# Mixer kernel on one core: the first channel product in half-height tiles, in one section a chunk

## The chip, the cores and the metric

The kernel runs on one core of one Trainium2 chip. The metric is the device time of one execution in microseconds (us). Before the change it is 2170.19 us, the median of three runs (2169.47 to 2170.86).

## The reference, cut to what matters

All tensors are given in float64. x is 8 x 4096 x 192, weight_gen 8 x 4096 x 8 x 7, and the result has the shape of x.

```python
w = softmax(weight_gen)                                  # over the 7 taps
out = sum over k of w[..., k] * x[:, s - 6 + k, group]   # 8 groups of 24 channels
# then, with x = out:
xt = x.transpose(0, 2, 1)
h = np.maximum(xt @ w_tok1, 0.0) @ w_tok2                # 4096 -> 256 -> 4096
u = x + h.transpose(0, 2, 1)
h2 = np.maximum(u @ w_ch1, 0.0) @ w_ch2                  # 192 -> 1536 -> 192
return (u + h2).astype(np.float32)
```

## The kernel before, in words

The tokens of each of the 8 batches are cut into 8 chunks of 512, so there are 64 chunks (g). For each chunk the kernel runs: the attention (a sum of seven weighted, shifted copies of x, on VectorE, called DVE, with DMAs that add into `xa`); `token1`, this chunk's part of the first token product, summed over the batch in `h1s`; once a batch's eight parts are there, `make_h1`; `token2`, the second token product for one chunk, which gives u; `channel1`, the first channel product; and `channel2`, the second, which sums into `acc`. `store` turns the sum and writes it out. Attention and token1 run about a batch ahead of the rest.

To keep float32 precision with fp32r matmuls, an operand is held as a high part and the low rest, and a product is three matmuls: high by high, low by high, high by low. `u_parts` makes these parts of u: a high part by ScalarE (ACT), a low part by DVE.

The 192 channels of u are the rows that a first-product matmul sums over. 128 of them (`a_hi`, `a_lo`) go through full-height matmuls (L578); the other 64 (`c_hi`, `c_lo`, held twice, in rows 0 to 63 and 64 to 127) through half-height ones (L583), of which two, for two different feature blocks, run in the two halves of the array at the same time. The 12 feature blocks of 128 are six pairs; a pair fills one PSUM tile `ph` (two banks). `channel1(g, q)` computes three pairs, q = 0 or 1: 18 full-height matmuls, then 9 pairs of half-height ones. ACT then takes max(ph, 0) into h (L586) and DVE the low rest (L587). Between the two sections of a chunk stands the second product of the section before, 30 full-height matmuls (L599), and a token2 or token1.

PSUM has eight banks: two for `acc`, and three working tiles of two banks (`ps_w`), shared in turn by `ph`, token2's `up` and token1's `th`. ACT copies x into `up` (L527) and u into `acc` (L607) first, so the matmuls add to them.

The order of the work is written out by the program when it is built: a planner keeps a modelled time per engine (`at`), with fixed costs for each piece, and lets TensorE's sections follow each other; `pump` fills DVE and ACT with items of waiting chains (attention, softmax, weight conversions, `u_parts`, output moves) up to a limit; `picks` says which token product comes next. Each engine then executes its queue in that order. The weights come as float64 and are converted on the chip, w1 and the first pieces of the others in a prologue, the rest in the first chunks.

Of the kernel before, what the change touches and what calls it, by code (L numbers as in the profile page):

```python
# [21 lines left out]
def mixer_kernel(ctx: ExitStack, tc: tile.TileContext, x, wg, wt1, wt2, wc1, wc2, out):  # L22
# [185 lines left out]
    def attention(ms):  # L208
# [29 lines left out]
        for ks in (TAPS if ms[0] >= EARLY * NCH else TAPS0):  # L238
# [209 lines left out]
    def convert_channel(which, n, pool=None):  # L448
# [4 lines left out]
        if which == "w1a":  # L453
            cs = slice(n * HF, (n + 1) * HF)
            yield from split(w1a_hi[:, cs], w1a_lo[:, cs], v)
# [91 lines left out]
    def u_parts(m):  # L547
# [3 lines left out]
        a_hi, a_lo, c_hi, c_lo = (late.tile([P, N], F32R, tag=x, name=x) for x in ("a_hi", "a_lo", "c_hi", "c_lo"))  # L551
        yield "gate", 0, lambda: state["channel1"] >= m * NQ
        yield "w", 0, lambda: free["parts"]
        yield "u", 620, lambda: nc.scalar.copy(a_hi, ua)
        yield "u", 620, lambda: nc.scalar.copy(c_hi[c], uc[c])
        yield "v", 610, lambda: nc.vector.tensor_sub(a_lo, ua, a_hi.bitcast(F32))  # L556
        yield "v", 610, lambda: nc.vector.tensor_sub(c_lo[c], uc[c], c_hi[c].bitcast(F32))
        yield "u", 620, lambda: nc.scalar.copy(c_hi[e], uc[c])
        yield "u", 620, lambda: nc.scalar.copy(c_lo[e], c_lo[c].bitcast(F32))

        def last():
            ut[m] = a_hi, a_lo, c_hi, c_lo
# [6 lines left out]
    def channel1(g, q):  # L569

        a_hi, a_lo, c_hi, c_lo = ut[g]
        pairs = range(PQ * q, PQ * (q + 1))
        ph = {p: ps_w.tile([P, 2, 512], F32, tag="w", name="ph") for p in pairs}
        for p in pairs:
            for j in range(2):
                fs = slice((2 * p + j) * P, (2 * p + j + 1) * P)
                for n, (w, u) in enumerate(((w1a_hi, a_hi), (w1a_lo, a_hi), (w1a_hi, a_lo))):
                    nc.tensor.matmul(ph[p][:, j, :], w[:, fs], u, start=n == 0, stop=False)  # L578
        for p in pairs:
            for n, (w, u) in enumerate(((w1c_hi, c_hi), (w1c_lo, c_hi), (w1c_hi, c_lo))):  # L580
# [9 lines left out]

    def channel2(g, q):
        acc = acc_t[g]
        for p in range(PQ * q, PQ * (q + 1)):
            h = ht.pop((g, p))
            for j in range(2):
                f = 2 * p + j
                for n, steps in ((1, ((C_HL, 0), (C_HL, 1))), (0, ((A_HI, 0), (A_LO, 0), (A_HI, 1)))):
                    for i, (d, l) in enumerate(steps):
                        nc.tensor.matmul(acc[:, n, :], w2s[:, f, d], h[:, j, l, :], start=False,  # L599
                                         stop=f == NF - 1 and i == len(steps) - 1, skip_group_check=True)  # L600
# [155 lines left out]
    def next_lo():
# [303 lines left out]
```

## Time and profile before

| what | value |
|---|---|
| median of three runs | 2170.19 us |
| profiled execution | 2166.28 us |
| its span, first to last instruction | 2164.5 us |
| TensorE busy | 2110.9 us (98%) |
| DVE busy | 1542.7 us (71%) |
| ACT busy | 1274.6 us (59%) |
| mean granted TensorE clock, share of full speed | 0.994 |

PE is TensorE's matmuls and PEld its weight loads, which run beside them. A busy share is a mean over the whole span, and TensorE's records overlap where matmuls are pipelined, so a matmul's pace is read from the starts of successive ones. In the timeline, successive equal instructions are one row with their count; the time of the row is from the first start to the last end.

### The profile page before, as it was taken

The page shows a single profiled execution, that of the slowest core. Times are in us where ns is not written, and L with a number is a line of the kernel's source. Part 1 is how long each engine was busy: PE and PEld are TensorE (multiplying, and loading weights), DVE is VectorE, ACT ScalarE, POOL GpSimd, SP SyncE. Part 2 cuts the span into 40 slices and gives each one's busy share as a digit, 9 for nine tenths or more (in the row PEclk, how much of TensorE's full clock was granted, in tenths as well). Part 3 has the DMA queues.
Part 4 walks back from the last instruction along what each step waited for, and adds up shares of the span by engine and source line. Part 5 has one row for each costly group of instructions (what it writes and reads, how often), then busy time and mean ns, then how long its engine had stood idle before and what let it go on. Part 6 is the DMA issues. An engine that isn't in the chain of part 4 may idle for free.

```text
span 2164.5 us, 27209 instructions
## 1 busy us (share of the span) xinstructions
PE 2110.9 (98%) x10438; PEld 1678.7 (78%) x10438; DVE 1542.7 (71%) x1749; ACT 1274.6 (59%) x1972; POOL 166.5 (8%) x202
## 2 busy tenths in 40 slices
PE   7988999899999999999999999999999999999998
PEld 5766788678778788878887888888788878877776
DVE  8988887788887887777777778777778764343342
ACT  5566664556655655665665566556656655655554
POOL 0001111000100010000100010000000000000000
PEclk9999999999999999999999999999999999999999
DMA  8666768777876677655766676566667553222211
GB/s 277 228 215 199 188 166 235 236 223 197 219 212 182 183 201 194 174 155 171 195 176 185 181 185 154 176 187 184 182 174 199 148 166 107 69 68 69 58 38 22
DMA packets 165826, 366.66 MB, mean 169 GB/s; under 512 B 16456, under 2 KB 104264, under 8 KB 150336
## 3 DMA queue, kind: packets, MB, share of 16 engines
q1 hardware_dynamic: 138304, 285.74, 41.2%
q0 software_dynamic: 26496, 77.61, 18.7%
q8 instruction: 82, 1.34, 0.2%
q10 hardware_dynamic: 896, 1.57, 0.2%
q14 instruction: 48, 0.39, 0.1%
HBM read 225.13 MB, written 70.52 MB: 137 GB/s over the span
## 4 chain that ended last, share of the span: by engine, by line
PE 86%; DVE 6%; DMA 3%; ACT 3%; issue 1%; POOL 0%; SPq 0%; ACTq 0%; DVEq 0%; POOLq 0%
PE acc L599 36%; PE ph L578 21%; PE ph L583 12%; PE up L533 6%; PE tapsum L342 3%; PE th L499 3%; PE th L501 1%; PE th L516 1%; DVE pr L215 1%; DVE h L587 1%; DMA xa<-pr 1%; DMA xs<-t 1%; DMA xt<-in_x_dram 1%; ACT h L586 1%; DVE pr L229 1%
## 5 line engine op out<-in xcount | busy, mean ns | idle before, releaser
L599 PE MATMUL acc<-h,w2s 128*128 128x512 f32 x3840 | 908.5, 393 | 0.0
L599 PEld LDWEIGHTS acc<-h,w2s 128*128 128x128 f32 x3840 | 711.0, 188 | 189.9 <-issue 45.7
L587 DVE SCALAR_TENSOR_TENSOR h<-ph,h 128x1024 fp32r<-128x1024 f32 x384 | 452.9, 1216 | 254.8 <-ACT h L586 252.4
L586 ACT ACTIVATE h<-ph 128x1024 fp32r<-128x1024 f32 x384 | 379.9, 1025 | 389.9 <-PE ph L583 225.4
L578 PE MATMUL ph<-a_hi,w1a_hi 128*128 128x512 f32 x768 | 303.8, 396 | 16.6 <-DVE uf L545 7.7
L215 DVE TENSOR_TENSOR pr<-xt,wn 128x768 f32<-128x768 f32 x336 | 309.2, 947 | 8.5 <-DMA xa<-pr 8.5
L578 PE MATMUL ph<-a_lo,w1a_hi 128*128 128x512 f32 x768 | 300.5, 391 | 1.1 <-DVE a_lo L556 1.1
L578 PE MATMUL ph<-a_hi,w1a_lo 128*128 128x512 f32 x768 | 300.4, 391 | 0.0
L233 POOL DMA_DIRECT2D xa<-pr x176 | 153.0, 870 | 1420.5 <-DVE pr L229 1195.0
L626 ACT COPY out_tile<-oa 32x256 f32<-32x256 f32 x512 | 206.7, 404 | 6.2
L607 ACT COPY acc<-uf 128x1024 f32<-128x1024 f32 x64 | 65.1, 1018 | 246.0 <-DVE oc L617 246.0
L578 PEld LDWEIGHTS ph<-a_hi,w1a_hi 128*128 128x128 f32 x768 | 145.1, 189 | 50.9 <-DVE uf L545 11.7
L578 PEld LDWEIGHTS ph<-a_lo,w1a_hi 128*128 128x128 f32 x768 | 144.7, 188 | 32.8 <-DVE a_lo L556 2.6
L533 PE MATMUL up<-w,h 128*128 128x512 f32 x630 | 157.2, 397 | 10.4 <-ACT up L527 10.4
L578 PEld LDWEIGHTS ph<-a_hi,w1a_lo 128*128 128x128 f32 x768 | 145.2, 189 | 27.9
L583 PE MATMUL ph<-c_hi,w1c_hi 64*128 64x512 f32 x768 | 165.1, 427 | 0.0
L229 DVE TENSOR_TENSOR pr<-pr 128x768 f32<-128x768 f32 x160 | 152.5, 953 | 3.5
L583 PE MATMUL ph<-c_lo,w1c_hi 64*128 64x512 f32 x768 | 151.8, 392 | 0.0
L583 PE MATMUL ph<-c_hi,w1c_lo 64*128 64x512 f32 x768 | 149.9, 387 | 0.0
L533 PEld LDWEIGHTS up<-w,h 128*128 128x128 f32 x630 | 120.3, 192 | 37.1 <-ACT up L527 12.0
L583 PEld LDWEIGHTS ph<-c_hi,w1c_hi 64*128 64x128 f32 x768 | 71.7, 183 | 56.2 <-issue 44.5
L545 DVE TENSOR_TENSOR uf<-up,uf 64x512 f32<-64x512 f32 x63 | 43.0, 683 | 99.0 <-ACT uf L541 99.0
(82 smaller groups left out, 2043.6 us busy)
## 6 DMA issues: line engine op xcount, KB each, us to landing
w<-s SPq DMA_DIRECT2D x96, 1024.0 KB, 5.1
xa<-pr POOLq DMA_DIRECT2D x176, 384.0 KB, 4.9
xt<-in_x_dram SPq DMA_DIRECT2D x56, 960.0 KB, 7.7
out_dram<-out_tile SPq DMA_DIRECT2D x128, 192.0 KB, 2.5
xs<-t SPq DMA_DIRECT2D x58, 384.0 KB, 3.9
xb<-xs SPq DMA_DIRECT2D x348, 64.0 KB, 4.1
raw<-in_moe_w_tok_dram SPq DMA_DIRECT2D x16, 1024.0 KB, 6.0
s<-w POOLq DMA_DIRECT2D x8, 1024.0 KB, 6.3
```

Source lines behind the costliest of these rows:

```text
L215: nc.vector.tensor_mul(t.rearrange("p t (h g) -> p (t h) g", h=H).rearrange("p (o n) g -> p o n g", o=1), x_k, w)
L229: nc.vector.tensor_add(sums[m], sums[m], prt.pop(m))
L233: nc.gpsimd.dma_start(xat[m].rearrange("p t d -> p (t d)"), sums[m].rearrange("p t d -> p (t d)"), accum_op=ALU.add)
L342: nc.tensor.matmul(ps[:, n, 0:half * D], ident, prs[k][:, n * half:(n + 1) * half, :], start=k == 0, stop=k == K - 1)
L533: nc.tensor.matmul(up[:, n, :], h1[:, k, d], w[:, l, k * N:(k + 1) * N], start=k == 0 and j == 0 and not seeded, stop=k == KR - 1 and j == ...
L578: nc.tensor.matmul(ph[p][:, j, :], w[:, fs], u, start=n == 0, stop=False)
L583: nc.tensor.matmul(ph[p][:, j, :], w[rows, p * P:(p + 1) * P], u[rows], start=False, stop=n == 2)
L586: nc.scalar.activation(h[:, :, 0, :], ph[p], AF.Relu)
L587: nc.vector.scalar_tensor_tensor(h[:, :, 1, :], ph[p], 0.0, h[:, :, 0, :].bitcast(F32), op0=ALU.max, op1=ALU.subtract)
L599: nc.tensor.matmul(acc[:, n, :], w2s[:, f, d], h[:, j, l, :], start=False, stop=f == NF - 1 and i == len(steps) - 1, skip_group_check=True)
L607: nc.scalar.copy(acc_t[g], uft.pop(g))
L626: nc.scalar.copy(dst, src[to:to + Q].rearrange("p (n e d) -> p n e d", n=2, d=Q)[:, n])
```

## The change

All 192 channels go through half-height matmuls, as three blocks of 64. `u_parts` puts them into `u_hi` and `u_lo`, three columns of 512 with rows 0 to 63 and 64 to 127 holding the same three blocks, the first two swapped between the halves; w1 is laid out to match. A pair is now 9 x 2 half-height matmuls. All six pairs of a chunk stand in one section. Four h tiles take pairs 0 to 3 at once; pairs 4 and 5 stay in PSUM until the second product has used the first two h tiles (`take_h`). One token product, token2 of the next chunk if it is ready, comes behind the section; then the second product's six pairs, with another token product in their middle. The planner's costs and limits for these pieces are new. The split of taps 5 and 6 for the second batch is gone. Lines of the changed kernel are numbered anew: the first product is L576, the second L594, token2 L527, token1 L493 and L495 (L510 in the first two batches), the seed of up L521, Relu L582 and the low rest L583.

```diff
-    TAPS0 = [(0,), (1, 2), (3, 4), (5,), (6,)]
...
-    w1a_hi = const.tile([P, F], F32R, name="w1a_hi")
-    w1a_lo = const.tile([P, F], F32R, name="w1a_lo")
-    w1c_hi = const.tile([P, F // 2], F32R, name="w1c_hi")
-    w1c_lo = const.tile([P, F // 2], F32R, name="w1c_lo")
+
+
+    w1_hi = const.tile([P, 3, F // 2], F32R, name="w1_hi")
+    w1_lo = const.tile([P, 3, F // 2], F32R, name="w1_lo")
+    TURN = (0, 1, 2), (1, 0, 2)
...
-        for ks in (TAPS if ms[0] >= EARLY * NCH else TAPS0):
+        for ks in TAPS:
...
+        if which == "w1":
+            dst = raw[:, 0:HF, :].rearrange("p (k q n) l -> p k q (n l)", k=3, q=NC1)
+            src = wc1.rearrange("(k c) (q j n) -> k j c q n", k=3, q=NP, j=2)[:, :, :, NC1 * n:NC1 * (n + 1)]
             for j in range(2):
-                nc.sync.dma_start(
-                    raw[j * DC:(j + 1) * DC, 0:HF, :].rearrange("p (q n) l -> p q (n l)", q=NP),
-                    wc1[DA:D].rearrange("c (q j n) -> c q j n", q=NP, j=2)[:, :, j, :])
+                for k in range(3):
+                    nc.sync.dma_start(dst[j * DC:(j + 1) * DC, k], src[TURN[j][k], j])
...
-        yield "u", 620, lambda: nc.scalar.copy(a_hi, ua)
-        yield "u", 620, lambda: nc.scalar.copy(c_hi[c], uc[c])
-        yield "v", 610, lambda: nc.vector.tensor_sub(a_lo, ua, a_hi.bitcast(F32))
-        yield "v", 610, lambda: nc.vector.tensor_sub(c_lo[c], uc[c], c_hi[c].bitcast(F32))
-        yield "u", 620, lambda: nc.scalar.copy(c_hi[e], uc[c])
-        yield "u", 620, lambda: nc.scalar.copy(c_lo[e], c_lo[c].bitcast(F32))
+        yield "u", 620, lambda: act(hi[:, 0], ua)
+        yield "u", 620, lambda: act(hi[c, 2], uc[c])
+        yield "v", 610, lambda: dve(lo[:, 0], ua, hi[:, 0].bitcast(F32))
+        yield "v", 610, lambda: dve(lo[c, 2], uc[c], hi[c, 2].bitcast(F32))
+        yield "u", 620, lambda: act(hi[c, 1], ua[e])
+        yield "u", 620, lambda: act(hi[e, 1], ua[c])
+        yield "u", 620, lambda: act(hi[e, 2], uc[c])
+        yield "u", 620, lambda: act(lo[c, 1], f[e, 0])
+        yield "u", 620, lambda: act(lo[e, 1], f[c, 0])
+        yield "u", 620, lambda: act(lo[e, 2], f[c, 2])
...
-    def channel1(g, q):
-
-        a_hi, a_lo, c_hi, c_lo = ut[g]
-        pairs = range(PQ * q, PQ * (q + 1))
-        ph = {p: ps_w.tile([P, 2, 512], F32, tag="w", name="ph") for p in pairs}
-        for p in pairs:
+    def channel1(g, p):
+
+        u_hi, u_lo = ut[g]
+        ph = ps_w.tile([P, 2, 512], F32, tag="w", name="ph")
+        steps = [(w, u, k) for w, u in ((w1_hi, u_hi), (w1_lo, u_hi), (w1_hi, u_lo)) for k in range(3)]
+        for n, (w, u, k) in enumerate(steps):
             for j in range(2):
-                fs = slice((2 * p + j) * P, (2 * p + j + 1) * P)
-                for n, (w, u) in enumerate(((w1a_hi, a_hi), (w1a_lo, a_hi), (w1a_hi, a_lo))):
-                    nc.tensor.matmul(ph[p][:, j, :], w[:, fs], u, start=n == 0, stop=False)
-        for p in pairs:
-            for n, (w, u) in enumerate(((w1c_hi, c_hi), (w1c_lo, c_hi), (w1c_hi, c_lo))):
-                for j in range(2):
-                    rows = slice(j * DC, (j + 1) * DC)
-                    nc.tensor.matmul(ph[p][:, j, :], w[rows, p * P:(p + 1) * P], u[rows], start=False, stop=n == 2)
-        for p in pairs:
-            h = ht[g, p] = late.tile([P, 2, 2, N], F32R, tag="h", name="h", bufs=5)
-            nc.scalar.activation(h[:, :, 0, :], ph[p], AF.Relu)
-            nc.vector.scalar_tensor_tensor(
-                h[:, :, 1, :], ph[p], 0.0, h[:, :, 0, :].bitcast(F32), op0=ALU.max, op1=ALU.subtract
-            )
-
-    def channel2(g, q):
+                rows = slice(j * DC, (j + 1) * DC)
+                nc.tensor.matmul(ph[:, j, :], w[rows, k, p * P:(p + 1) * P], u[rows, k], start=n == 0,
+                                 stop=n == len(steps) - 1)
...
+    def take_h(g, p, ph):
+        h = ht[g, p] = late.tile([P, 2, 2, N], F32R, tag="h", name="h", bufs=HB)
+        nc.scalar.activation(h[:, :, 0, :], ph, AF.Relu)
+        nc.vector.scalar_tensor_tensor(
+            h[:, :, 1, :], ph, 0.0, h[:, :, 0, :].bitcast(F32), op0=ALU.max, op1=ALU.subtract
+        )
...
-    C1, C2 = 6570, 6820
-    LAST = 690
-    FIRST = 1362
+    PAIR, C2 = 2065, 2272
+    TIGHT4 = 900
+    TIGHT = 1100
...
+    for g in range(NG):
+        phs, kept = {}, {}
+        soon = ((convert_w2, 1),) if g == 0 else ()
+        for p in range(NP):
+            if g == 0 and p == 2 * NC1:
+                need(lambda: ("w1", 2) in done)
+            if p < HB:
+                slack = TIGHT if p < NP // 2 else TIGHT
+                pump(next_lo() + slack, soon, first_h() + slack - TIGHT)
+            phs[p] = channel1(g, p)
+            end = on("pe", PAIR, w_at.popleft(), free["u"] if p == 0 else 0.0)
+            if p < HB:
+                take_h(g, p, phs[p])
+                w_at.append(on("dve", LOW, on("act", TOP, end)))
+                if p == 0:
+                    h_at = w_at[-1]
+            else:
+                kept[p - HB] = end + T2 + (p - HB + 1) * C2 + TOP + LOW
+                w_at.append(kept[p - HB])
+        picked = list(picks(g, 100, 1))
+        state["channel1"] = g + 1
+        state["rest"] = NP * C2
+        free["parts"] = end
+        run_picked(picked)
+        for p in range(NP):
+            if p == NP // 2:
+                if not picked:
+                    if g < NCH - 1 and state["token2"] <= g:
+                        need(lambda: g + 1 in w2t, (convert_w2, g + 1))
+                    picked = list(picks(g, 2000, 2))
+                if not picked:
+                    pump(at["pe"] + SLACK)
+                    picked = list(picks(g, 100, 2))
+                run_picked(picked)
+                if g == 0:
                     need(lambda: ("c2", 2) in done, (convert_channel, "c2", 2))
...
+            channel2(g, p)
+            on("pe", C2, free["acc"] if p == 0 else 0.0, h_at)
+            state["rest"] -= C2
+            if p + HB < NP:
+                pump(at["pe"] + TOP + SLACK, soon, at["pe"])
+                last = p + HB == NP - 1
+                if last:
+                    it = picks(g, (NP // 2 - p - 1) * C2, 2)
+                    picked = list(islice(it, 1))
+                take_h(g, p + HB, phs[p + HB])
+                h_at = on("dve", LOW, on("act", TOP, at["pe"]))
+                if kept[p] in w_at:
+                    w_at[w_at.index(kept[p])] = h_at
+                if last:
+                    picked += list(it)
+                    h_at = 0.0
+        pump(at["pe"] + SLACK_M)
+        need(lambda: state["stored"] >= g - 1, ("o", g - 1))
+        items = store(g)
+        next(items)
+        free["acc"] = on("dve", 1400, at["pe"] + HOP, stored_at.get(g - 1, 0.0))
+        chains.insert(3, Chain(items, 0.0, ("o", g)))
...
```

The first place is TensorE's queue in a chunk of the fourth batch, before: the end of one section's half-height matmuls, the second product, token2 and the start of the next section.

```order
L583 MATMUL ph<-c_hi,w1c_hi 128x512 x2
L583 MATMUL ph<-c_hi,w1c_lo 128x512 x2
L583 MATMUL ph<-c_lo,w1c_hi 128x512 x2
L599 MATMUL acc<-h,w2s 128x512 x30
L533 MATMUL up<-w_7112,h_6987 128x512 x10
L578 MATMUL ph<-a_hi,w1a_hi 128x512
```

The same queue after, in the same batch: the last pair of the section, token2, the second product and token1.

```order
L576 MATMUL ph<-u_hi,w_hi 128x512 x6
L576 MATMUL ph<-u_hi,w_lo 128x512 x6
L576 MATMUL ph<-u_lo,w_hi 128x512 x6
L527 MATMUL up<-w_8132,h_8056 128x512 x10
L594 MATMUL acc<-h,w2s 128x512 x30
L493 MATMUL th<-xh,w_7834 128x384
L495 MATMUL th<-xh,w_7834 128x192
```

Token2 has moved ahead of the second product, and TensorE changes between half and full height twice a chunk instead of four times.

The second place is DVE's queue in a chunk of that batch, before, from the transposes of the store (L616, L617) over token2's last step (L545) and attention steps (L215, L229) to the three low rests of a section.

```order
L616 STREAM_TRANSPOSE oa<-acc 128x512
L617 STREAM_TRANSPOSE oc<-acc 128x512
L619 TENSOR_TENSOR oc<-oc 64x512
L545 TENSOR_TENSOR uf<-up,uf 64x512
L229 TENSOR_TENSOR pr<-pr 128x768
L215 TENSOR_TENSOR pr<-xt,wn 128x768 x2
L229 TENSOR_TENSOR pr<-pr 128x768
L181 TENSOR_REDUCE mx<-wg 128x64
L182 TENSOR_TENSOR wg<-wg,mx 128x448
L587 SCALAR_TENSOR_TENSOR h<-ph,h 128x2x512 x3
```

After, in the fuller of the two kinds of chunk that alternate there (in the other, nothing stands between the first three low rests):

```order
L611 STREAM_TRANSPOSE oa<-acc 128x512
L612 STREAM_TRANSPOSE oc<-acc 128x512
L614 TENSOR_TENSOR oc<-oc 64x512
L214 TENSOR_TENSOR pr<-xt,wn 128x768 x2
L583 SCALAR_TENSOR_TENSOR h<-ph,h 128x2x512
L228 TENSOR_TENSOR pr<-pr 128x768
L583 SCALAR_TENSOR_TENSOR h<-ph,h 128x2x512
L214 TENSOR_TENSOR pr<-xt,wn 128x768
L583 SCALAR_TENSOR_TENSOR h<-ph,h 128x2x512
L214 TENSOR_TENSOR pr<-xt,wn 128x768
L583 SCALAR_TENSOR_TENSOR h<-ph,h 128x2x512
```

Four low rests instead of three stand behind the store, with an attention step between them, and token2's last step (now L539) has moved behind them.

The third place is TensorE's queue at the end of chunk 7, where the second batch's token1 is completed; before and after.

```order
L599 MATMUL acc<-h,w2s 128x512 x30
L516 MATMUL th<-xa,val 128x192 x16
L533 MATMUL up<-w_2379,h_2789 128x512 x10
L578 MATMUL ph<-a_hi,w1a_hi 128x512
L578 MATMUL ph<-a_hi,w1a_lo 128x512
```

```order
L594 MATMUL acc<-h,w2s 128x512 x30
L510 MATMUL th<-xa,val 128x192 x8
L527 MATMUL up<-w_2717,h_3157 128x512 x10
L576 MATMUL ph<-u_hi,w_hi 128x512 x6
L576 MATMUL ph<-u_hi,w_lo 128x512 x6
```

Token2 stands directly ahead of the next first product in both; one token1 instead of two stands ahead of it.

## Rows read from the trace of the kernel before

**Rows 1.** The page: busy shares, chain by line, two groups (busy us, mean ns).

```profile
PE 2110.9 (98%) x10438; PEld 1678.7 (78%) x10438; DVE 1542.7 (71%) x1749; ACT 1274.6 (59%) x1972; POOL 166.5 (8%) x202
...
PE acc L599 36%; PE ph L578 21%; PE ph L583 12%; PE up L533 6%; PE tapsum L342 3%; PE th L499 3%; PE th L501 1%; PE th L516 1%; DVE pr L215 1%; DVE h L587 1%; DMA xa<-pr 1%; DMA xs<-t 1%; DMA xt<-in_x_dram 1%; ACT h L586 1%; DVE pr L229 1%
...
L587 DVE SCALAR_TENSOR_TENSOR h<-ph,h 128x1024 fp32r<-128x1024 f32 x384 | 452.9, 1216 | 254.8 <-ACT h L586 252.4
L586 ACT ACTIVATE h<-ph 128x1024 fp32r<-128x1024 f32 x384 | 379.9, 1025 | 389.9 <-PE ph L583 225.4
```

**Rows 2.** Stretches: us, busy of PE, PEld, DVE, ACT, POOL; granted clock, DMA.

```profile
118.00:426.00 308.00, 283.79 (x1366) 223.09 (x1364) 249.29 (x289) 186.82 (x279) 38.42 (x47) 0.97 0.73 203
426.00:750.00 324.00, 317.66 (x1598) 254.11 (x1596) 264.40 (x310) 195.96 (x306) 32.02 (x37) 1.00 0.73 202
750.00:1750.00 1000.00, 1000.00 (x5039) 805.43 (x5036) 749.59 (x877) 597.54 (x939) 86.44 (x100) 1.00 0.65 180
```

**Rows 3.** TensorE's waits: total us, times, longest us.

```profile
PE up L533 <- ACT up L527: 10.4, 4, 4.5
PE ph L578 <- DVE uf L545: 7.7, 8, 1.7
```

**Rows 4.** TensorE's timeline, steady part: start us, us, instruction.

```profile
1499.83 0.39 PE L578 MATMUL ph<-a_lo,w1a_hi 128*128 128x512 f32 x1
1500.14 0.50 PE L583 MATMUL ph<-c_hi,w1c_hi 64*128 64x512 f32 x2
1500.48 0.40 PE L583 MATMUL ph<-c_hi,w1c_lo 64*128 64x512 f32 x2
1500.71 0.40 PE L583 MATMUL ph<-c_lo,w1c_hi 64*128 64x512 f32 x2
1500.95 0.40 PE L583 MATMUL ph<-c_hi,w1c_hi 64*128 64x512 f32 x2
...
1502.10 0.40 PE L583 MATMUL ph<-c_lo,w1c_hi 64*128 64x512 f32 x2
1502.43 7.10 PE L599 MATMUL acc<-h,w2s 128*128 128x512 f32 x30
1509.37 0.33 PE L499 MATMUL th<-xh,w 128*128 128x384 f32 x1
1509.54 0.25 PE L501 MATMUL th<-xh,w 128*128 128x192 f32 x1
1509.63 0.36 PE L499 MATMUL th<-xh,w 128*128 128x384 f32 x1
...
1511.87 0.40 PE L578 MATMUL ph<-a_hi,w1a_lo 128*128 128x512 f32 x1
...
1515.51 0.39 PE L578 MATMUL ph<-a_lo,w1a_hi 128*128 128x512 f32 x1
```

**Rows 5.** Timeline of DVE and ACT, 600 to 640 us.

```profile
600.76 1.82 DVE L215 TENSOR_TENSOR pr<-xt,wn 128x768 f32<-128x768 f32 x2
...
605.60 1.02 ACT L527 COPY up<-xb 128x1024 f32<-128x1024 f32 x1 [1.73 <-DVE h L587]
...
610.47 0.71 DVE L616 STREAM_TRANSPOSE oa<-acc 128x512 f32<-128x512 f32 x1
...
611.82 0.69 DVE L619 TENSOR_TENSOR oc<-oc 64x512 f32<-64x512 f32 x1
...
624.37 0.62 ACT L554 CAST a_hi<-uf 128x512 fp32r<-128x512 f32 x1
```

**Rows 6.** TensorE's timeline at the end of chunk 7.

```profile
396.41 2.59 PE L533 MATMUL up<-w,h 128*128 128x512 f32 x10 [2.09 <-ACT up L527]
400.97 0.51 PE L578 MATMUL ph<-a_hi,w1a_hi 128*128 128x512 f32 x1 [1.97 <-ACT a_hi L554]
```

**Rows 7.** SP's timeline in the prologue (it issues DMAs).

```profile
19.70 0.69 SPq L433 DMA_DIRECT2D raw<-in_moe_w_ch_dram  x1
29.03 0.33 SPq L370 DMA_DIRECT2D raw<-in_moe_w_tok_dram  x1
```

More of the change, by code (lines that the diff above doesn't have):

```diff
@@ L35, in mixer_kernel @@
     NP = NF // 2
-    PQ = 3
-    NQ = NP // PQ
+    NC1 = NP // 3
+    HB = 4
     KR = R // P
@@ L452, in convert_channel @@
         v, = out
-        if which == "w1a":
-            cs = slice(n * HF, (n + 1) * HF)
-            yield from split(w1a_hi[:, cs], w1a_lo[:, cs], v)
+        if which == "w1":
+            cs = slice(n * NC1 * P, (n + 1) * NC1 * P)
+            yield from split(w1_hi[:, :, cs], w1_lo[:, :, cs], v.rearrange("p (k m) -> p k m", k=3))
         elif which == "c2":
@@ L591, in channel2 @@
-    def channel2(g, q):
-        acc = acc_t[g]
[L593 to L600, printed above, removed]
+    def channel1(g, p):
[3 more added lines that the diff above has]
+        for n, (w, u, k) in enumerate(steps):
+            for j in range(2):
+                rows = slice(j * DC, (j + 1) * DC)
+                nc.tensor.matmul(ph[:, j, :], w[rows, k, p * P:(p + 1) * P], u[rows, k], start=n == 0,
+                                 stop=n == len(steps) - 1)
+        return ph
@@ new lines, in take_h, with channel2 @@
+    def take_h(g, p, ph):
[4 more added lines that the diff above has]
+        )
+    def channel2(g, p):
+        acc = acc_t[g]
+        h = ht.pop((g, p))
+        for j in range(2):
+            f = 2 * p + j
+            for n, steps in ((1, ((C_HL, 0), (C_HL, 1))), (0, ((A_HI, 0), (A_LO, 0), (A_HI, 1)))):
+                for i, (d, l) in enumerate(steps):
+                    nc.tensor.matmul(acc[:, n, :], w2s[:, f, d], h[:, j, l, :], start=False,
+                                     stop=f == NF - 1 and i == len(steps) - 1, skip_group_check=True)
@@ L752, in first_h @@
     def first_h():
-        return max(at["pe"], *(t - i * FIRST for i, t in enumerate(w_at))) + C1 - (PQ - 1) * LAST
+        return max(at["pe"] + state["rest"], w_at[0]) + PAIR
     def next_lo():
@@ L764, in mixer_kernel @@
              "summed": NCH - 1, "turned": FT - 1, "parts": NCH - 1, "kept": FT - 1, "stored": -1, "out": -1,
-             "done": NCH - 1, "w1": NCH, "channel1": 0}
+             "done": NCH - 1, "w1": NCH, "channel1": 0, "rest": 0}
     def raw_free(tag):
@@ L836, in start @@
             return items
-        between = {1: ("w1a", 0), 3: ("w1c", 0), 5: ("c2", 0)}
+        between = {1: ("w1", 0), 3: ("w1", 1), 5: ("c2", 0)}
         w1_v, w1_it = {}, {}
@@ L891, in mixer_kernel @@
         make_h1(0, th[:, :, 0:D])
-        last = start(convert_channel("w1a", 1))
+        last = start(convert_channel("w1", 2))
         soft = softmaxes()
@@ L908, in mixer_kernel @@
         for j in range(2):
-            nc.tensor.matmul(w[:, j, :], w1a_hi[:, 0:P], w1a_hi[:, 0:512], start=True, stop=True)
+            nc.tensor.matmul(w[:, j, :], w1_hi[:, 0, 0:P], w1_hi[:, 0, 0:512], start=True, stop=True)
     run(u_parts(0))
@@ L967, in token2_ready, with picks @@
             and h1_at[m // NCH] <= at["pe"] + soon
-    def picks(g, soon):
+    def picks(g, soon, most):
         two = token2_ready(g + 1, soon)
@@ L973, in picks, with run_picked @@
             yield do_token2, begin_token2(g + 1)
[L974 removed]
+        if two < most and token1_ready(soon) and ready[0][0] <= g + NCH + (2 if not two else BEHIND):
             yield do_token1, begin_token1()
+    def run_picked(picked):
+        for do, it in picked:
+            do(*it)
+        picked.clear()
     seed(0)
[L978 to L1030 removed]
@@ new lines, in mixer_kernel @@
+    for g in range(NG):
[33 more added lines that the diff above has]
+                if g == 0:
+                    need(lambda: ("c2", 2) in done, (convert_channel, "c2", 2))
+            channel2(g, p)
[20 more added lines that the diff above has]
+        chains.insert(3, Chain(items, 0.0, ("o", g)))
+        if g + 1 == NG:
+            break
+        if state["token2"] < g + 1:
+            while (g + 1) // NCH not in h1t:
+                need(token1_ready, ("w1", state["token1"] + 1), ("x", state["token1"] + 1))
+                do_token1(*begin_token1())
+            need(lambda: g + 1 in w2t and g + 1 in xbt, (convert_w2, g + 1))
+            do_token2(*begin_token2(g + 1))
+        need(lambda: g + 1 in ut, ("u", g + 1))
+        seed(g + 1)
+        free["acc"] = on("act", 1050, free["acc"])
```

77 lines of the change are left out of this document (9 added, 68 removed).

## The prediction

> **What bounds the kernel now.** I read the page first. TensorE is busy for 98% of the span, VectorE (DVE) for 71% and ScalarE (ACT) for 59%, and the chain that ended last runs above all through the second channel product (L599, 36%) and the first (L578 and L583, 33%) [rows 1]. Then I read the busy time by stretch, because a mean hides where TensorE waits. From 750 to 1750 us it is busy 1000 us of 1000: there the time is the TensorE instruction stream and nothing else. From 118 us, where the chunks begin, to 426 us it is idle 24.2 us, and from there to 750 us another 6.3 us [rows 2]. In the first of these the granted clock is 0.97 on average: with two levels, 1.2 and 2.4 GHz, that is some 6% of 308 us, about 18 us, at the lower one, which costs about 9 us. The waits say for whom: longest in total for the ACT copy that seeds token2's PSUM tile, and eight times for DVE's last step of u (L545), on which the first channel product waits [rows 3]. So two things can be gained: TensorE's own slots (everywhere), and the waits before 750 us.
>
> **TensorE's slots.** By a slot I mean what streams 512 columns once: one full-height matmul, or two half-height ones that start together (the rows show them as x2). A chunk has 2 x (18 + 9) = 54 slots of the first product before, and 6 x 9 = 54 after: the multiplication is not made cheaper. A full-height slot takes (1515.51 - 1511.87) / 16 = 0.2275 us, a half-height one (1502.10 - 1500.48) / 7 = 0.2314 us [rows 4]. What differs is how often TensorE changes between the two heights. Into half height: 0.31 us from 1499.83 to 1500.14 is 0.083 over a slot, and 0.34 to the next is 0.109 over. Back: 0.33 from 1502.10 to 1502.43 is 0.099 over, and the thirty L599 slots take 6.94 instead of 30 x 0.2275 = 6.825, 0.115 more [rows 4]. A round trip thus costs 0.406 us. Before there are two a chunk, after one, as the order shows: 64 x 0.406 = 26.0 us gone. Against it, 36 full-height slots a chunk become half-height ones: 36 x (0.2314 - 0.2275) x 64 = 9.0 us added. Net gain 17.0 us.
> The half-height pace in a run of 54 slots is not shown; the trace has runs of nine. From below I bound it by the full-height pace, 0.2275 (gain 26.0 + 64 x 18 x 0.0039 = 30.5), from above by the slowest single step, 0.24 between 1500.71 and 1500.95 [rows 4]: then 64 x (36 x 0.0125 + 18 x 0.0086) = 38.7 us are added and the net is a loss of 12.7. I take 0.2314, the mean, since the steps do not grow towards the end of the nine.
>
> **Where the new order could make TensorE wait, in the steady part.** The three working PSUM tiles now hold six pairs in a row: pair 3 needs the tile of pair 0, and token2's seed (ACT, L521 in the new numbering) needs the tile of pair 3. I set t = 0 at the first half-height slot. Pair p is complete at about 0.3 + 2.08 (p + 1), and the product ends at about 12.7. Take the fuller of the two kinds of chunk, the one whose DVE order is shown. DVE starts its transposes at 0.2; the three steps of the store take 2.04 (610.47 to 611.82 + 0.69) and two attention products 1.82 [rows 5], so the first h step starts at 4.1; each takes 1.22 [rows 1], each attention step between them 0.87, as the second of the two in 1.82 does [rows 5]. The h steps end at 5.3, 7.4, 9.5 and 11.5. Tiles are wanted at 6.4, 8.4 and 10.5, so pairs 3 to 5 start on time with about 1 us to spare. The seed takes 1.02 [rows 5] and ends at about 12.65, against 12.7: just in time. ACT has four Relu passes at 1.02 [rows 1] and two seeds of 1.02 there, 6.1 of 12.7 us, and output moves in the rest. I take no wait; its other bound is one more DVE step of 0.95 in each chunk of this kind.
> What the order gains: token2 now comes directly behind the product, before the 13.6 us of the second product, so u's evictions and casts are long done at the next chunk. The eight waits for L545, 7.7 us [rows 3], go. The four casts that are added (0.62 each [rows 5], 64 x 4 x 0.62 = 159 us on ACT, 59% to 66%) lie in that time at no cost. They cost something where token2 still ends its chunk, below.
>
> **The early part, 118 to 750 us.** Here DVE is 81% busy [rows 2] and also converts the weights. Pairing taps 5 and 6 for the second batch too adds eight adds (0.87 each, 7 us of DVE) and takes eight accumulating DMAs away; none of it is on the path, but DVE has less slack. Going through the DVE queue in its new order with the durations above, I find waits for PSUM tiles of 1 to 4 us in chunks 1 to 5, because DVE enters the product late with weight conversions or attention left over; the old places fall away. In chunk 0 the third part of w1 is now wanted for pair 4 instead of the second half, 2 us later. Chunk 7 still ends in the last token1 and token2 directly before the next product: its waits of 2.09 and 1.97 us [rows 6] stay, and as the first pair's nine slots now need all eight casts, 6 x 0.62 = 3.7 us behind the first two against 8 x 0.23 = 1.9 of slots, it loses 1.9 us more, about 2 more for DVE's backlog behind it, and the 1.9 once more in chunk 0. Together I put the idle time of 118 to 426 us at 18 instead of 24.2 us, the loss by the lower clock at 5 instead of 9 (it is 1.00 in the stretches with fewer waits [rows 2]), and 426 to 750 us at 2 instead of 6.3: 14.5 us gained. This is the weak term; its bounds are nothing and all of it, 0 to 39 us.
> The loads of w1: 18 DMAs instead of 4, of 64 partitions each. At 0.69 us of SP for one, each of three places takes some 3.5 us longer; behind the first of them SP idles from 20.4 to 29.0 us until a buffer comes free [rows 7], so it is hidden. If that cover went, a raw tile would come 3.5 us later, and TensorE's chain in the prologue would see at most that.
>
> **Sum.** 17.0 + 14.5 = 31.5 us. The profiled execution took 2166.3 us (span 2164.5 and 1.8 around it), so it would be 2134.8; the median of the runs is 2170.2, 3.9 above the profiled one, and the forecast on that scale is 2138.7 us.
>
> **Rivals.**
> 1. The slots gain and the waits only move: 2170.2 - 17.0 = 2153. For it: DVE's work in the early part is not less, and it was 81% busy there. Against: the waits for L545 have a cause that the new order removes.
> 2. Slower, by token2's seed. The chain fourth pair, Relu, h step, seed has no slack to spare in the fuller chunks. If DVE comes one step of 0.95 later in all of the 52 chunks with attention work, TensorE waits 49 us in front of token2 (L527) and the kernel takes 2138.7 + 49 = 2188. It decides from 31.5 / 52 = 0.6 us per chunk on. Against: every second chunk's queue has no attention step between its h steps, and DVE idles 25% of the steady part [rows 2].
> 3. The half-height pace does not hold over 54 slots, as each has two loads and two matmuls, four instructions in 0.23 us. Break-even lies at 0.2314 + 31.5 / (64 x 54) = 0.2405 us; at the upper bound of 0.24 the time is 2168, no change. Against: in token1 a load and a matmul fit into 0.09 us (1509.54 to 1509.63 [rows 4]), twice as fast as needed; but that is one step in two, not a long run. The Trainium skill, "TensorE: Matmul & The Clock Gate", Part 2, has a rule that speaks against the change: where the sequencer decodes matmuls itself, it spends about 62 ns on each. The two matmuls of a slot would need 124 ns and stay hidden; only if the loads cost as much would a slot take 0.248 us by that figure, and the kernel about 2196, an estimate. The 0.09 us above is against this.
> 4. Nearly all waits go: 17.0 + 35 = 52 us, 2118.
>
> **How the numbers follow.** The forecast has 0.56 (2125 to 2148 by half of its weak term), rival 1 0.20, rival 4 0.06, rivals 2 and 3 together 0.18, of which 0.05 end within 0.2% (4.3 us, about what a measurement of this kernel can tell from no change) and 0.13 above. So faster 0.82, same 0.05, slower 0.13. The range, 2120 to 2163, takes in the forecast and rival 1 and leaves out most of rivals 2 to 4.
>
> **What would show it.** Right: the steady chunk shrinks from 31.35 us (1000 x 158 matmuls of a chunk / 5039 [rows 2]) to about 31.1 with TensorE still without idle time; one step of 0.3 us into half height a chunk; no waits for L539 (the old L545); idle time before 426 us near 18 us, with the longest at the start of chunk 8. Wrong: waits of L527 for ACT L521 in every second chunk (rival 2), half-height steps of 0.24 us or more (rival 3), or waits of L576 for DVE L583 that go on after 500 us.

## The result, and the profile after

The changed kernel takes 2177.81 us (median of 6 runs, 2177.03 to 2179.45), the kernel before beside it 2170.55 (6 runs, 2169.47 to 2171.16): a ratio of 1.0035, 95% interval 1.0022 to 1.0048. It is slower by 0.35%, where I forecast 2138.7.

The page of the profiled execution: span, then busy us, share of the span and instructions of an engine.

```profile
span 2175.6 us, 32133 instructions
PE 2100.8 (97%) x12742; PEld 1701.2 (78%) x12742; DVE 1548.5 (71%) x1757; ACT 1437.0 (66%) x2228; POOL 157.8 (7%) x194
```

ACT has the four casts a chunk that were added (59% to 66%, against [rows 1]). The same three stretches as in [rows 2]:

```profile
118.00:426.00 308.00, 286.75 (x1698) 231.49 (x1697) 258.20 (x299) 210.89 (x319) 31.23 (x39) 0.97 0.68 195
426.00:750.00 324.00, 307.61 (x1882) 249.38 (x1882) 260.85 (x308) 210.92 (x328) 31.64 (x37) 0.98 0.72 200
750.00:1750.00 1000.00, 986.22 (x6135) 808.33 (x6132) 737.71 (x864) 677.62 (x1066) 84.54 (x99) 0.99 0.64 175
```

Before, TensorE had no idle time from 750 to 1750 us; now it has 13.8 us there and 16.4 from 426 to 750 (6.3 before), and the clock is below 1.00 in both. Its waits (engine, tile and line, whom it waits for: us in total, times, longest) say who was late:

```profile
PE ph L576 <- DVE h L583: 26.0, 12, 5.3
PE up L527 <- ACT up L521: 8.5, 13, 2.3
PE ph L576 <- ACT u_hi L553: 6.7, 4, 2.6
```

And one of DVE's own waits:

```profile
DVE t L294 <- DMA xa<-pr: 21.1, 8, 4.2
```

The waits of [rows 3] for L545 are gone. In their place the fourth pair's slots wait for DVE's first h step, which frees its PSUM tile. Most of it comes in a few chunks. By the distance from one chunk's first slot of L576 to the next one's, an ordinary chunk takes 30.89 us (31.34 before) and one of the last eight, which have no token1, 28.60 (29.05 before). But chunks 24, 32 and 40 (counted from 0; a batch has eight) take 35.1 to 35.2 us and chunk 48 takes 36.8; chunks 8 to 16 lose most. In sums, with 6.93 us added to each start but the first of before and of every kernel in two sections, where the second half of the last chunk's product still follows:

| chunks | before | changed | planner mended | and less slack |
|---|---|---|---|---|
| 0 to 7 | 284.1 | 281.4 | 280.9 | 282.1 |
| 8 to 16 | 292.1 | 306.3 | 288.2 | 285.9 |
| 17 to 55 | 1223.7 | 1226.6 | 1209.7 | 1204.3 |
| 56 to 62 | 203.4 | 200.2 | 200.2 | 200.2 |

(The last two columns are experiments, below.) An ordinary chunk gains 0.45 us; chunks 8 to 16 lose 14.2 us, and behind them the first chunks of the batches (24, 32, 40 and 48) take back what the ordinary chunks win.

The slots themselves, in TensorE's timeline of a steady chunk:

```profile
1502.33 0.84 PE L576 MATMUL ph<-u_hi,w_lo 64*128 64x512 f32 x6
...
1511.17 0.84 PE L576 MATMUL ph<-u_lo,w_hi 64*128 64x512 f32 x6
1511.94 2.58 PE L527 MATMUL up<-w,h 128*128 128x512 f32 x10
```

From 1502.33 to 1511.17 there are 39 slots: 0.2267 us each, no more than the full-height 0.2275 of [rows 4]. The way out costs 0.77 - 0.68 = 0.09 us.

Now a batch end: the start of chunk 24, the first of a batch. First DVE, then ACT, then TensorE; the bracket holds the idle time ahead of the instruction and whom it waited for.

```profile
930.54 0.98 DVE L294 STREAM_TRANSPOSE t<-xa 128x768 f32<-128x768 f32 x1 [2.55 <-DMA xa<-pr]
931.44 0.67 DVE L611 STREAM_TRANSPOSE oa<-acc 128x512 f32<-128x512 f32 x1
...
932.75 0.69 DVE L614 TENSOR_TENSOR oc<-oc 64x512 f32<-64x512 f32 x1
933.47 0.62 DVE L183 TENSOR_REDUCE mx<-wg 128x64 f32<-128x448 f32 x1
...
934.95 0.96 DVE L189 TENSOR_TENSOR wn<-wg,mx 128x448 f32<-128x448 f32 x1
935.82 2.35 DVE L583 SCALAR_TENSOR_TENSOR h<-ph,h 128x1024 fp32r<-128x1024 f32 x2
```

```profile
932.75 1.02 ACT L602 COPY acc<-uf 128x1024 f32<-128x1024 f32 x1 [3.99 <-DVE oc L612]
933.70 1.02 ACT L582 ACTIVATE h<-ph 128x1024 fp32r<-128x1024 f32 x1
```

```profile
928.32 0.97 PE L576 MATMUL ph<-u_hi,w_hi 64*128 64x512 f32 x6
...
933.91 0.84 PE L576 MATMUL ph<-u_lo,w_hi 64*128 64x512 f32 x6
937.10 0.96 PE L576 MATMUL ph<-u_hi,w_hi 64*128 64x512 f32 x6 [2.34 <-DVE h L583]
937.89 0.94 PE L576 MATMUL ph<-u_hi,w_lo 64*128 64x512 f32 x6
938.62 1.49 PE L576 MATMUL ph<-u_lo,w_hi 64*128 64x512 f32 x6
939.90 1.49 PE L576 MATMUL ph<-u_hi,w_hi 64*128 64x512 f32 x6
941.18 1.21 PE L576 MATMUL ph<-u_hi,w_lo 64*128 64x512 f32 x6
942.24 0.86 PE L576 MATMUL ph<-u_lo,w_hi 64*128 64x512 f32 x6
```

DVE takes its instructions in order. The one at its head is a transpose whose input an accumulating DMA still writes; DVE stands for 2.55 us, and behind it stand the three steps of the store, four softmax steps and then the first h step. ACT is late by the same wait: its copy of u into acc (L602) stands for 3.99 us until the store's second transpose is done, and the Relu that the first h step needs comes behind it and ends at 934.7. The h step starts at 935.82, where TensorE wanted its tile from 934.6 on and needs the step's 1.2 us as well: it waits 2.34 us. From 938.6 on, three slots take 1.28 us and not 0.68. Chunks 16, 32, 40 and 48 show the same order on DVE, with waits of 2.5 to 4.2 us for this DMA.

### The profile page after: what moved, and what is told of

Its sections match the earlier page's. It is cut to its first block, busy times and chain, and to the rows that moved or that the text cites. A ratio compares the mean times of both kernels' runs of the same rounds, so it can differ in the third digit from the quotient of the medians.

```text
span 2175.6 us, 32133 instructions
## 1 busy us (share of the span) xinstructions
PE 2100.8 (97%) x12742; PEld 1701.2 (78%) x12742; DVE 1548.5 (71%) x1757; ACT 1437.0 (66%) x2228; POOL 157.8 (7%) x194
## 5 line engine op out<-in xcount | busy, mean ns | idle before, releaser
L594 PE MATMUL acc<-h,w2s 128*128 128x512 f32 x3840 | 893.8, 390 | 2.6 <-DVE w2s L457 2.5
L594 PEld LDWEIGHTS acc<-h,w2s 128*128 128x128 f32 x3840 | 716.5, 188 | 150.9 <-DVE w2s L457 2.9
L583 DVE SCALAR_TENSOR_TENSOR h<-ph,h 128x1024 fp32r<-128x1024 f32 x384 | 465.9, 1218 | 149.2 <-ACT h L582 149.0
L582 ACT ACTIVATE h<-ph 128x1024 fp32r<-128x1024 f32 x384 | 392.8, 1025 | 103.6 <-PE ph L576 64.8
L576 PE MATMUL ph<-u_hi,w_hi 64*128 64x512 f32 x2304 | 348.8, 401 | 35.2 <-DVE h L583 26.0
L576 PE MATMUL ph<-u_lo,w_hi 64*128 64x512 f32 x2304 | 336.2, 392 | 0.0
L576 PE MATMUL ph<-u_hi,w_lo 64*128 64x512 f32 x2304 | 336.2, 392 | 0.0
L576 PEld LDWEIGHTS ph<-u_hi,w_hi 64*128 64x128 f32 x2304 | 219.3, 188 | 107.6 <-DVE h L583 31.6
L602 ACT COPY acc<-uf 128x1024 f32<-128x1024 f32 x64 | 65.1, 1017 | 339.4 <-DVE oc L612 339.4
L576 PEld LDWEIGHTS ph<-u_hi,w_lo 64*128 64x128 f32 x2304 | 225.3, 188 | 47.4
L576 PEld LDWEIGHTS ph<-u_lo,w_hi 64*128 64x128 f32 x2304 | 224.9, 187 | 47.0 <-ACT u_lo L557 0.6
L539 DVE TENSOR_TENSOR uf<-up,uf 64x512 f32<-64x512 f32 x63 | 42.9, 681 | 225.4 <-ACT uf L535 225.4
L527 PE MATMUL up<-w,h 128*128 128x512 f32 x630 | 162.8, 405 | 8.7 <-ACT up L521 8.5
L527 PEld LDWEIGHTS up<-w,h 128*128 128x128 f32 x630 | 114.8, 189 | 52.7 <-ACT up L521 21.4
L521 ACT COPY up<-xb 128x1024 f32<-128x1024 f32 x63 | 64.0, 1016 | 90.0 <-DVE h L583 90.0
L493 PE MATMUL th<-xh,w 128*128 128x384 f32 x384 | 112.6, 358 | 1.0 <-ACT th L486 0.8
L621 ACT COPY out_tile<-oc 32x256 f32<-32x256 f32 x256 | 103.2, 403 | 15.5 <-DVE oc L614 10.9
L272 DVE TENSOR_TENSOR xh<-xa,xh 128x768 fp32r<-128x768 f32 x48 | 45.8, 955 | 78.7 <-ACT xh L269 78.7
```

What stands on the lines that cost most here:

```text
L493: nc.tensor.matmul(th[:, r, 0:2 * D], w[:, c, 0, rs], xh[:, c, :], start=i + c == 0, stop=False, skip_group_check=True)
L521: nc.scalar.copy(up.rearrange("p k (n b c) -> p (k n) c b", c=CT, b=Q), xb.rearrange("p k (n c b) -> p (k n) c b", c=CT, b=Q))
L527: nc.tensor.matmul(up[:, n, :], h1[:, k, d], w[:, l, k * N:(k + 1) * N], start=k == 0 and j == 0 and not seeded, stop=k == KR - 1 and j == ...
L576: nc.tensor.matmul(ph[:, j, :], w[rows, k, p * P:(p + 1) * P], u[rows, k], start=n == 0, stop=n == len(steps) - 1)
L582: nc.scalar.activation(h[:, :, 0, :], ph, AF.Relu)
L583: nc.vector.scalar_tensor_tensor(h[:, :, 1, :], ph, 0.0, h[:, :, 0, :].bitcast(F32), op0=ALU.max, op1=ALU.subtract)
```

## Theory and rivals

The order on DVE is written by the kernel's own planner. In the new loop the planner keeps one time, `h_at`, for which the second product's pairs wait: pair 0's h step at first, then the last one issued, and nothing once pair 5's is out. Behind pair 0 it issues the h step of pair 4, so pair 1 is made to wait for pair 4's h step, where the chip waits for pair 1's, long done. By the constants of the code that is TOP + HOP + LOW + HOP = 1000 + 60 + 1180 + 60 = 2.3 us a chunk that do not exist, more where the model has ACT or DVE still busy: the planner's chunk is at least 6 x 2065 + 6 x 2272 + 2264 + 2270 + 2300 ns = 32.9 us, the chip's 30.89. Before, the same sum, 2 x 6570 + 2 x 6820 + 2264 + 2270 ns = 31.3, is what the chip takes. **Theory A**: with 2.3 us too much a chunk, the planner hands DVE work too early by TensorE's real time and by that of the DMAs, and DVE stands in front of data that has not landed, with the h steps behind. **Theory B**: the long section, with three PSUM tiles and four hidden tiles for six pairs, has too little room whatever the order. **Others**: the 64-row tiles and their casts; the retuned numbers of the diff (KEEP, SLACK, tap groups).

## Experiments

**The planner mended (plan_from_chunk9).** TensorE's and DVE's work is the same, only the order is another.

```diff
-            on("pe", C2, free["acc"] if p == 0 else 0.0, h_at)
+            on("pe", C2, free["acc"] if p == 0 else 0.0, h_at[HB] if p == 1 and g < OLD else h_at[p])
...
-                h_at = on("dve", LOW, on("act", TOP, at["pe"]))
+                h_at[p + HB] = on("dve", LOW, on("act", TOP, at["pe"]))
```

(OLD is 9: the first nine chunks, 0 to 8, keep the old rule.)

> Edit: in the planner alone, the second channel product of pair 1 waits for pair 1's own hidden tile and no longer for that of pair 4, from the ninth chunk on; the planner's modelled steady chunk falls from 33.1 to 30.6 us (the chip takes 30.9), and the order on DVE and ACT changes with it. Theory A (the slots gained what they should, and the loss is an order of DVE's queue made by a clock that counts 2.3 us too much a chunk): the 4.2 us lost at each of the four batch ends and most of the 13 us lost over chunks 9 to 17 go; 2150 us, at most 2162. Theory B (the long section with three PSUM tiles and four hidden tiles has too little room whatever the order): the waits only move, 2170 to 2180.

2140.72 us, less than either theory had; against before on the same chip (2168.74) a ratio of 0.9871, interval 0.9855 to 0.9887. (The expectation's 33.1 is the planner's clock with its waits for ACT and DVE, where 32.9 is the sum of the constants.) TensorE's waits and stretches:

```profile
PE up L527 <- ACT up L521: 7.3, 9, 2.3
...
PE ph L576 <- DVE h L583: 5.9, 9, 1.7
```

```profile
118.00:426.00 308.00, 286.63 (x1698) 228.75 (x1698) 257.98 (x299) 211.76 (x320) 31.23 (x39) 0.97 0.69 197
426.00:750.00 324.00, 319.36 (x1989) 261.88 (x1988) 268.38 (x317) 227.72 (x353) 31.66 (x37) 1.00 0.76 207
750.00:1750.00 1000.00, 996.07 (x6248) 817.59 (x6248) 748.10 (x878) 686.00 (x1073) 85.42 (x100) 1.00 0.66 179
```

The wait for the h step falls from 26.0 to 5.9 us and the idle time after 426 us from 30.2 to 8.6. DVE's wait of 21.1 us for the accumulating DMA is gone from the list. Theory A holds, and theory B falls: tiles and loop are the same. So are the 64-row tiles, their casts and the retuned numbers: none of them keeps the kernel slow once the planner is mended.

**The transpose alone, later (turn_later).**

```diff
-            yield "w", 0, lambda: max(xa_at.get(m, 0.0), free["t"])
+            yield "w", 0, lambda: max(xa_at.get(m, 0.0) + TURN_LATE, free["t"])
...
+    TURN_LATE = 3500
```

> Edit: the planner alone takes the transpose of the attention sum to be possible 3.5 us later than the accumulating DMA's modelled end, so that at a batch's end DVE reaches it behind the three steps of the store and no longer ahead of them. Theory A: DVE's wait at a batch's end falls from 2.5 to about 0.5 us, the seed of acc is no longer behind it, and the batch ends cost 1 us and not 4.2: 2160 to 2168. Theory B: the store, the transpose, four softmax steps and the first hidden step stand in one row on DVE all the same, so the first hidden step stays late: 2174 to 2180.

2147.15 us, ratio 0.9902 (0.9887 to 0.9916): a larger gain than expected. The planner's clock stays wrong, but the one instruction that suffered from it at a batch's end has moved, and the batch ends cost 0.6 us (chunks of 31.5) instead of 4.2. Chunks 8 to 16 take 295.6 us, between 306.3 and 288.2.

**The fault put into the kernel before (before_long_clock).**

```diff
                 on("pe", C2, h_at.pop(prev), free["acc"] if prev[1] == 0 else 0.0)
+                at["pe"] += PHANTOM if prev[1] == 0 else 0
...
+    PHANTOM = 2300
```

> Edit to the kernel before: its planner's TensorE clock is set 2.3 us ahead once a chunk (behind the first half of the second channel product), nothing else. Theory A: the kernel before loses as the changed one does, 8 to 25 us: 2178 to 2195. Theory B (the planner's clock is not what costs): within 3 us of 2170.5.

2193.47 us, ratio 1.0120 (1.0099 to 1.0141), 25 us lost. Chunks 8 to 16 take 312.1 us and not 292.1, and DVE shows the same picture, a step that stands for an accumulating DMA ahead of three h steps:

```profile
1352.91 0.96 DVE L215 TENSOR_TENSOR pr<-xt,wn 128x768 f32<-128x768 f32 x1 [4.65 <-DMA xa<-pr]
1353.79 3.48 DVE L587 SCALAR_TENSOR_TENSOR h<-ph,h 128x1024 fp32r<-128x1024 f32 x3
```

TensorE pays for it at other places than in the changed kernel: its wait for the h step stays at the 2.5 us of before, and token2's seed and u's last step are late (10.4 and 7.7 us in [rows 3]):

```profile
PE up L533 <- ACT up L527: 16.7, 7, 4.5
...
PE ph L578 <- DVE uf L545: 9.4, 11, 1.8
```

So the clock costs by itself, with full-height tiles, two sections and five hidden tiles.

**The retuned numbers undone (constants_back).**

```diff
-    KEEP = 9500
+    KEEP = 6000
-    SLACK = 1500
+    SLACK = 2500
-        for ks in TAPS:
+        for ks in (TAPS if ms[0] >= EARLY * NCH else TAPS0):
```

> Edit to the changed kernel: three of its retuned numbers as in the kernel before (the time after which the transpose's tile is free 6.0 and not 9.5 us, the slack in front of a pumped step 2.5 and not 1.5 us, the tap groups of the first two batches), its planner's clock left as it is. Theory A (the planner's clock is what costs): it stays slow, 2170 to 2195. Rival (the retuned numbers cost it): 2140 to 2155.

2192.27 us, ratio 1.0121 (1.0106 to 1.0136). The wait for the h step grows (two added lines make L583 into L585 here):

```profile
PE ph L578 <- DVE h L585: 43.0, 26, 7.1
```

The retuned numbers are not what costs; under the long clock they save some 15 to 19 us (by the medians, by the two ratios).

**64-row tiles in the loop of before (half_rows_two_sections).**

```diff
-                for n, (w, u) in enumerate(((w1a_hi, a_hi), (w1a_lo, a_hi), (w1a_hi, a_lo))):
...
+        steps = [(w, u, k) for w, u in ((w1_hi, u_hi), (w1_lo, u_hi), (w1_hi, u_lo)) for k in range(3)]
...
-            h = ht[g, p] = late.tile([P, 2, 2, N], F32R, tag="h", name="h", bufs=5)
+            h = ht[g, p] = late.tile([P, 2, 2, N], F32R, tag="h", name="h", bufs=4)
```

> Edit to the kernel before: the first channel product in 64-row tiles alone (the changed kernel's weights, feature parts and slots, 27 slots a section), in the loop of before with its two sections a chunk; four hidden tiles in place of five, for room. Slots: 54 a chunk in both; two switches a chunk stay. If the 64-row pace is 0.2265 us from the tenth slot on, as the changed kernel's trace shows, a chunk gains 0.05 to 0.1 us: 2163 to 2171. If the 64-row tiles or their four more casts a chunk are what made the changed kernel slow: 2176 or more.

2333.13 us, ratio 1.0758 (1.0742 to 1.0775). That is on the side of the second expectation but far beyond it, and it does not show that the 64-row tiles or the casts are what costs, for the experiment had two edits in it: the larger feature parts had left room for four hidden tiles only. So four hidden tiles were tried alone, and the 64-row tiles with five.

> Edit to the kernel before: four hidden tiles in place of five, nothing else (a control for the run with 64-row tiles in two sections, which took 2333 and not 2163 to 2171). Theory C (with four hidden tiles in a two-section loop the second and third relu of a section wait for pairs of the second channel product, and ACT's casts of the next features stand behind them): a wait of 1 to 2 us in a chunk, 2200 to 2300. Theory D (the 64-row pace or the four more casts cost it): within 5 us of 2169.

The control is one number, `bufs=5` to `bufs=4` in the kernel before: 2245.31 us, ratio 1.0352 (1.0337 to 1.0368), 77 us for one tile. ACT shows why:

```profile
2102.69 1.03 ACT L586 ACTIVATE h<-ph 128x1024 fp32r<-128x1024 f32 x1
2105.27 1.03 ACT L586 ACTIVATE h<-ph 128x1024 fp32r<-128x1024 f32 x1 [1.55 <-PE acc L599]
2107.54 1.03 ACT L586 ACTIVATE h<-ph 128x1024 fp32r<-128x1024 f32 x1 [1.24 <-PE acc L599]
2108.59 0.62 ACT L554 CAST a_hi<-uf 128x512 fp32r<-128x512 f32 x1
```

The second and the third Relu of a section wait until the second channel product gives a hidden tile back, and the casts of the next features stand behind them. TensorE then waits for u's last step (7.7 us in 8 waits before):

```profile
PE ph L578 <- DVE uf L545: 45.6, 29, 3.3
```

> Edit to the kernel before: 64-row tiles in two sections as in the run that took 2333, now with five hidden tiles, and three product tiles of the attention in place of four for the room. The last eight chunks hold no attention and are read apart from the rest: they were 31.1 us with four hidden tiles, 29.05 in before. Theory C (four hidden tiles): 29.0 to 29.1. Theory E (in two sections ACT has no room for four more casts between the sections): 29.6 to 31. Whole kernel by theory C, with up to 25 us for the missing product tile: 2165 to 2195.

Here `bufs=5` and `PR = 3` in place of 4: 2241.48 us, ratio 1.0346 (1.0329 to 1.0363), more than theory C allowed for the whole (theory E had no number for it). The last chunks go by theory C: 29.09 us against 29.05 of before. So 64-row tiles cost 0.04 us a chunk there, not 0.14, and going to one section (28.60) gains 0.49, in which one round trip between the heights is contained (I had worked out 0.406). With token1 in the chunk it is 31.71 and 32.95 in turn (31.34 before), and in every second chunk TensorE waits 0.7 to 1.8 us for a cast that stands behind two of the added ones:

```profile
PE ph L579 <- ACT u_hi L556: 18.1, 19, 1.8
```

So the casts can cost something in two sections where token1 is in the chunk: 18.1 us of waits, where 73 us are lost. This run too has a second edit: what the missing product tile costs, and whether these waits come without it, was not separated.

**Versions.** Three more start from the mended planner.

> Edit: the planner's wait for the hidden tile mended from the ninth chunk on, and the transpose taken to be possible 3.5 us later, both together. If they take away the same loss, the time is that of the better one, 2139 to 2143; if each leaves a part that the other takes (chunks 9 to 17 the one, 0.6 in place of 1.0 to 1.7 us a batch end the other), 2133 to 2139.

The two edits above together: 2143.61 us, ratio 0.9888 (0.9873 to 0.9903). They take away the same loss: chunks 17 to 55 take 1209.7 us, as with the planner mended alone.

> Edit: the planner's wait for the hidden tile mended in all chunks, and the tap groups of the first two batches as in the kernel before (one more accumulating DMA and one less DVE sum in a chunk). Theory A: what is left is in the first nine chunks, where DVE and the transfers set the pace, and a clock that runs too long there costs little: 2135 to 2148. If the too-long clock costs the first nine chunks as it did the later ones: 2120 to 2132.

`OLD = 0` and the tap groups of before: 2143.64 us, ratio 0.9886 (0.9871 to 0.9900). Chunks 1 to 6 now take 30.6 to 31.3 us and chunk 7 takes 59.4: chunk 8 starts 283.7 us after chunk 0, against 280.9. The early loss moves and does not go.

```diff
-    TIGHT = 1100
+    TIGHT = 600
```

> Edit: the planner's wait for the hidden tile mended from the ninth chunk on, and the first four hidden steps of a chunk allowed to be 0.6 us late by its clock and not 1.1 us. At the batch ends the fourth pair's slots still wait 0.5 to 0.85 us for the first hidden step, and two of five lose 1.3 us at the token product. If the slack is what is left, the batch ends fall from 1.0 to 1.7 us to under 0.7: 2134 to 2139. If the token product's seed takes its place, 2140 to 2144.

2136.39 us (4 runs, 2134.66 to 2141.38), ratio 0.9866 (0.9849 to 0.9883): the lowest median here, though the interval holds the 0.9871 of the mended planner too. What it gains on that one stands in the traces: 5.4 us in chunks 17 to 55. From 750 to 1750 us TensorE is busy throughout, with 6294 matmuls where the changed kernel had 6135:

```profile
750.00:1750.00 1000.00, 1000.00 (x6294) 821.54 (x6294) 758.32 (x882) 688.52 (x1080) 86.25 (x101) 1.00 0.69 180
```

At a batch's end attention steps, which have their data, now stand where the transpose and the softmax stood, and the h step is in time for pair 3 at 914.62, DVE first and TensorE below:

```profile
910.53 0.96 DVE L228 TENSOR_TENSOR pr<-pr 128x768 f32<-128x768 f32 x1
911.40 0.95 DVE L214 TENSOR_TENSOR pr<-xt,wn 128x768 f32<-128x768 f32 x1
912.27 1.22 DVE L583 SCALAR_TENSOR_TENSOR h<-ph,h 128x1024 fp32r<-128x1024 f32 x1
```

```profile
913.94 0.84 PE L576 MATMUL ph<-u_lo,w_hi 64*128 64x512 f32 x6
914.62 0.84 PE L576 MATMUL ph<-u_hi,w_hi 64*128 64x512 f32 x6
```

## Why the prediction was wrong

**TensorE's slots: right in kind, too small.** Forecast 17.0 us, measured 0.45 a chunk, some 28 over 63 chunks. The mis-sized term is the 9.0 us for the half-height pace: nine-slot runs gave 0.2314, a run of 54 gives 0.2267 after them. My bound with no penalty (30.5) was near; rival 3 is out. The Trainium skill ("TensorE: Matmul & The Clock Gate", Part 2) has 62 ns for each matmul that the sequencer decodes; by that figure for loads and matmuls alike a slot would be an estimated 0.248 us, and the trace's 0.2267 does not bear that out.

**The steady part, "I take no wait": this step failed.** It holds for the ordinary chunk. I had worked through the DVE queue of one kind of chunk, took each step as ready when its turn came, and never set the planner's constants against TensorE's time, though they stood in the code. In the first chunk of a batch other steps stand ahead of the h steps, and the first of them waits for a DMA; the term that I had put at nothing is 2.3 to 4.0 us of TensorE's waiting there. From chunk 17 to 55 some 20.4 us are taken back, most of it in chunks 24, 32, 40 and 48: the ordinary 0.45 in 39 chunks is 17.5, and the stretch is 2.9 longer than before.

**L545's eight waits go: right**; none is left for L539. **Four casts at no cost: right in the steady part**, where TensorE waits for no cast after chunk 8. In two sections, with one product tile less, it waited 18.1 us for them.

**The early part: failed too.** I forecast 18 us idle before 426 us (21.3 measured) and 2 from there to 750 (16.4). The planner's clock accounts for most of the second: mended, it is 4.6. The first does not answer to it (21.4 mended), nor did the clock recover there: 0.97, as before, where I had put its loss at 5 us in place of 9. Of 14.5 us forecast here, the mended kernel gains next to nothing: chunks 0 to 16 take 7.1 us less than before, and 0.45 in each of 17 chunks is 7.7. Chunk 7's end kept its wait of 1.97 us for u_hi, as forecast; behind it came another 0.86, where I had put 1.9. The same casts hold chunks 0, 1 and 2 up by 1.6, 1.7 and 2.6 us; of these I had counted the first alone.

```profile
405.50 0.50 PE L576 MATMUL ph<-u_hi,w_hi 64*128 64x512 f32 x2 [1.97 <-ACT u_hi L549]
406.86 1.95 PE L576 MATMUL ph<-u_hi,w_hi 64*128 64x512 f32 x4 [0.86 <-ACT u_hi L553]
```

**The loads of w1 hidden: right.** The first chunk starts at 124.1 us, 123.8 before.

**The rivals.** None named this. Rival 2 had the right side and the wrong place: the seed of token2 waits 8.5 us in all and 2.4 after 750 us, where I had taken none, and what is late is the h step at a chunk's start. The sign that I gave for being wrong, waits of L576 for L583 beyond 500 us, is what came: seven of over 2 us. That the mended kernel, at 2140.7, lands near my 2138.7 is no credit to the sum: its slots gain 11 us more and its early part some 14 less than I had put down.

## What stays open

The first nine chunks take 34 us (before), 39 (changed) and 41 (plan_all_taps_back) more than nine ordinary ones. The last of these moved the loss among the chunks; no run took it away, and what sets it was not measured by itself. Open too is what the 64-row tiles and their casts cost in a loop of two sections with all its tiles.

## What to carry to other kernels

Where a program orders in-order queues by its own clock, add up the clock's constants for one turn of the loop and set the sum beside the measured turn before anything else: here they were 32.9 and 30.9 us, and mending the one wait between them took 37 us off. Then read the order of the rare turn (a batch's end) as well as the common one, and ask of each step ahead of the critical one whether its data will have landed, not only how long it takes. An experiment with two edits in it explains little: the tile that was given up for room cost 77 us by itself, and what the part under test cost stayed open.

## What the hardware showed that I had not expected

A run of 64-row pairs is as fast as full-height matmuls (0.2267 and 0.2275 us for 512 columns); what cost in the ordinary chunk was the change between heights, about 0.1 us over a slot each time. And a wait can cost again after it has ended. The first row is the wait at the batch end above, the second the slots that begin 1.4 us later, the third what follows (the clock is the number before the last two):

```profile
934.80:937.10 2.30, 0.00 (x1) 0.00 (x2) 2.27 (x4) 2.23 (x5) 0.00 (x0) 1.00 1.01 416
938.50:942.20 3.70, 3.70 (x22) 2.94 (x20) 2.22 (x2) 1.82 (x3) 0.00 (x0) 0.54 0.38 92
942.90:946.00 3.10, 3.10 (x24) 2.27 (x21) 0.42 (x1) 3.00 (x7) 0.00 (x0) 1.00 0.00 0
```

The granted clock of 0.54 is the lower level, 1.2 of 2.4 GHz, for nearly all of these 3.7 us. Against 0.68 us for three slots, the nine from 938.62 to 942.24 take 3.62 instead of 2.04: 1.6 us on top of the 2.3. It is not so after every wait: behind the one of 2.59 us that ends at 687 us the clock stays at 1.00.
